# A Nystrom attention in front of a multiplicative FFN on one core: turnings from DMA and TensorE to VectorE, C v without zero blocks, other column blocks, another order

## The chip, the cores and the metric

The kernel runs on one core of a Trainium2 chip. The metric is device time in microseconds (us), from the first to the last instruction with what the runtime puts around them; lower is better. Engines are named as the profile names them: PE is TensorE (PEld its weight loads), DVE is VectorE, ACT is ScalarE, POOL is GpSimd, SP is SyncE, which here only issues transfers.

## The reference, cut to what matters

There are 8 batches of 8 heads, 576 tokens and 64 columns; 32 landmarks are means over 18 neighbouring tokens.

```python
q_lm = q.reshape(B, H, 32, 18, D).mean(axis=3)
k_lm = k.reshape(B, H, 32, 18, D).mean(axis=3)
A  = softmax(q    @ k_lm.T / 8)      # 576 x 32 for each head
Bm = softmax(q_lm @ k_lm.T / 8)      # 32 x 32
C  = softmax(q_lm @ k.T / 8)         # 32 x 576
Z = Bm.T / (norm_1(Bm) * norm_inf(Bm) + 1e-6)      # norms over rows and columns
for _ in range(6):
    Z = 2 * Z - Z @ Bm @ Z
x = (A @ Z @ C @ v)                  # heads side by side: 4608 x 512
out = ((x @ w1) * (x @ w2)) @ w3 @ w_out           # 512 -> 1024 -> 1024 -> 512, float32 out
```

## The kernel before, in words

**The dense half.** w3 and w_out are multiplied once, at the start, into one matrix w34 (1024 x 512). Both are split into a high and a low fp16 half (L303, L308, L324, L331) and three products are summed (`w34_mm`); w3 is turned beforehand by PE, four 128 x 128 blocks at a time (`w3_tr`, L317). x itself is never formed. For each batch the small matrix Z C v of each head is multiplied with w1 and w2 (`u_mm`, copied by `u_out`, L800), which gives u. Dense-1 (`d1_mm`) is then u times A, for 8 blocks j of 128 columns of the FFN and for 2 blocks of 288 tokens; ACT copies the first of the two products from PSUM (`d1_a`, L866) and DVE multiplies it with the second (`d1_b`, L872) into the tile ab. Dense-2 (`d2_mm`) multiplies ab with w34 for 128 tokens at a time, ACT copies the result out (L885) and SP stores it in four transfers (L895).

**The attention half.** It goes by quads, four heads of one batch, 16 in all. POOL's queue loads k and q as fp16 (`load_qk`, L391); SP turns the whole of it by a transposing DMA into the tile T (`trans`, L419). POOL sums the 18 tokens of each landmark in five steps (L427, L434) and scales the sum into a small tile with zero blocks (`mean_c`, L441, L445), which another transposing DMA turns (`lm_trans`, L452). PE then makes C's and Bm's scores in a bank of their own, psS (`s_mm`), and A's scores (`a_mm`: 40 matmuls of 128 rows, the landmarks standing in a matrix of which half is zero). C's maximum is shared between two halves of the partitions by a small matmul (`s_swap`), ACT makes its exponentials (L513), DVE turns them in blocks of 32 (L529), and POOL spreads the sums (L521). A goes through maximum, difference, exponential, sum and reciprocal (L555, L561, L570, L576, L577), POOL multiplies (L582), DVE turns it (L589) into the tile aT. Bm's scores are copied out (L489) and get a softmax of their own for each batch (L672 to L689). `cv_mm` multiplies C with v; v lies in a tile in which every second block of 64 columns is zero (`const_e` writes the zeros, L280, and `load_v` fills the others, L404). Five double steps of the iteration (`it_mm`, `it_out` L739) and three small products follow for each batch.

**The order of the work.** All instructions are tasks of a planner, the class `Plan`. It holds for each task an engine, an estimated duration, what it depends on, which slots of which rings of buffers it takes and frees, and a priority from a due time: `dense(b)` is 66 + 25.5 b, `att(n)` and `lane(b)` are derived from it. `run` makes a list schedule from these, and the kernel is written out in this order; each engine runs its own list strictly in order. The ring "P" has 6 of the 8 PSUM banks, psS has two. Nearly all matmuls are issued by the helper `mm` (L228), so they are told apart by their tiles. The tiles ab take the memory of the tiles of the w34 stage, so they begin when that is done.

Of the kernel before, what the change touches and what calls it, by code (L numbers as in the profile page):

```python
# [20 lines left out]
NC9 = 9  # L21
DM = 512
DF = 1024
HALF = 288
# [3 lines left out]
LOW = -1e30  # L28


class Task:
    def __init__(self, name, eng, dur, fn, deps, acq, rel, prio, mode, lat, move, after):
        self.name, self.eng, self.dur, self.fn = name, eng, dur, fn
        self.deps, self.acq, self.rel = deps, acq, rel
        self.prio, self.mode, self.lat, self.move, self.after = prio, mode, lat, move, after
        self.start = self.ready = None


class Plan:
# [3 lines left out]
    LAT = {"PE": 0.25, "ACT": 0.08, "DVE": 0.08, "POOL": 0.1, "SP": 0.0}  # L43
    SWITCH = 0.1
# [8 lines left out]
    def add(self, name, eng, dur, fn, deps=(), acq=(), rel=(), prio=0.0, mode=None, lat=None,  # L53
            move=0.0, after=0.0):
        t = Task(name, eng, dur, fn, list(deps), list(acq), list(rel), prio, mode,
                 self.LAT[eng] if lat is None else lat, move, after)
        self.by[name] = t
        self.tasks.append(t)
        return t

    def _slots(self, acq):

        got, when, taken = [], 0.0, {}
        for ring, key, n, uses in acq:
            free = self.rings[ring]
            used = taken.setdefault(ring, set())
            if n == 1:
# [3 lines left out]
                best = min(some, key=lambda i: (free[i], -(free[i ^ 1] is None) if ring == "P" else 0, i))  # L71
                pick = [best]
            else:
# [5 lines left out]
                best = min(some, key=lambda i: max(free[i], free[i + 1]))  # L79
# [5 lines left out]

    def run(self):
        free = {e: 0.0 for e in self.LAT}
        mode, moved = None, 0.0
        todo = list(self.tasks)
        waiting = {t.name: sum(1 for d in t.deps) for t in todo}  # L90
        after = {}
        for t in todo:
# [3 lines left out]
        for t in todo:  # L96
            if not waiting[t.name]:
                t.ready = 0.0
                avail[t.eng].append(t)
        order = []  # L100
        n = len(todo)
        while len(order) < n:
            best = None
            for e, cand in avail.items():
                opts = []
                for t in cand:
                    found = self._slots(t.acq)
                    if found is None:
                        continue
                    at = max(free[e], t.ready, found[0], t.after)  # L110
                    opts.append((at, t, found[1]))
                if not opts:
                    continue
                first = min(o[0] for o in opts)
                near = [o for o in opts if o[0] <= first + (0.05 if e == "PE" else 0.0)]
                at, t, got = min(near, key=lambda o: (
                    o[1].prio - (0.6 if e == "PE" and o[1].mode == mode else 0.0)))
                if best is None or at < best[0]:
                    best = (at, t, got)
            if best is None:  # L120
                left = [t.name for t in todo if t.start is None]
                raise RuntimeError(f"stuck with {len(left)}: {left[:12]} {self.rings}")
# [4 lines left out]
            dur = t.dur  # L127
            if e == "PE":
                if t.mode != mode:
                    dur += self.SWITCH  # L130
                mode = t.mode
            free[e] = at + dur
            end = at + dur + t.lat
            if t.move:
                moved = max(moved, at + dur) + t.move
                end = moved + t.lat
            t.end = end
# [5 lines left out]
            for key in t.rel:  # L143
                rec = self.left[key]
                rec[0] -= 1
                rec[1] = max(rec[1], end)
# [3 lines left out]
            for u in after.get(t.name, ()):  # L150
                waiting[u.name] -= 1
                if not waiting[u.name]:
                    u.ready = max(self.by[d].end for d in u.deps)
                    avail[u.eng].append(u)
            order.append(t)
        return order


@with_exitstack
def kernel(  # L160
# [18 lines left out]
    psS = banks[3]  # L179
# [8 lines left out]
    P.ring("P", 6)  # L188
    P.ring("S", 1)
    nats = slots(fixed, 4, [128, 2, GRP, D], FP16, "nat")  # L190
    Ts = slots(fixed, 3, [128, 2 * NC9, 128], FP16, "T")
    lsum = slots(fixed, 1, [128, 2, NC9, D], FP32, "ls")
    lm16 = slots(fixed, 2, [128, 3, 2, D], FP16, "lm")
    lmTs = slots(fixed, 3, [128, 3, 128], FP16, "lmT")
    vbs = slots(fixed, 4, [128, 2, 2, NC9, D], FP32, "vb")
    ecs = slots(fixed, 2, [128, 2, 2, 160], FP32, "ec")
    ecTs = slots(fixed, 4, [128, 2, 10, M], FP32, "ecT")
    eas = slots(fixed, 2, [128, GRP, M], FP32, "ea")
    ahs = slots(fixed, 2, [128, GRP, M], FP16, "ah")
    aTs = slots(fixed, 6, [128, S], FP16, "aT")  # L200
    uu = slots(fixed, 4, [128, 2, DF], FP16, "u")
    asb = slots(fixed, 4, [128, HALF], FP16, "asb")
    osb = slots(fixed, 4, [128, DM], FP32, "osb")
    bscs = slots(fixed, 2, [128, 2, 32], FP32, "bsc")
    wTs = slots(fixed, 2, [128, 2, 128], FP16, "wT")
    cvs = slots(fixed, 2, [128, 2, D], FP32, "cv")
    bms = slots(fixed, 2, [128, 2, 2, 32], FP32, "bm")
    xzs = slots(fixed, 4, [128, 2, 2, 32], FP32, "xz")
    zbs = slots(fixed, 2, [128, 2, 4, 32], FP32, "zb")
    tinies = slots(fixed, 8, [128, 48], FP32, "tiny")  # L210
# [6 lines left out]
    swapneg = fixed.tile([128, 2, 32], FP32, name="swapneg")  # L217
    blockones = fixed.tile([128, 128], FP32, name="blockones")
    ones = fixed.tile([128, 32], FP32, name="ones")
    maskS = fixed.tile([128, 2], FP32, name="maskS")  # L220
# [9 lines left out]


    T0 = 66.0
    PER = 25.5

    def dense(b):
        return T0 + PER * b

    def att(n):
        b, qd = divmod(n, 2)
        return max(2.0 + 6.0 * n, dense(b) - 46.0 + 13.0 * qd)  # L240

    def lane(b):
        return dense(b) - 19.0
# [9 lines left out]
    def const_c():  # L253
        nc.vector.memset(blockones, 0.0)
        nc.vector.memset(ones, 1.0)
        nc.vector.memset(swapneg, 0.0)
        nc.vector.memset(maskS, 0.0)
        for j in range(4):
# [6 lines left out]
            nc.vector.tensor_scalar(out=swapneg[r, 1 - j % 2, :], in0=ident[r, r], scalar1=-SCALE,  # L265
                                    scalar2=None, op0=ALU.mult)
        for s in range(2):
            nc.vector.memset(maskS[64 * s:64 * s + 64, s:s + 1], 1.0)
        for hp in range(2):
            nc.vector.memset(psS[:, 1, 160 * hp + 128:160 * hp + 160], LOW)  # L270

    def const_d():
        for t in lm16:
            nc.vector.memset(t, 0.0)

    def const_e(i):
        def fn():
            for t in vbs[2 * i:2 * i + 2]:
                for s in range(2):
                    nc.gpsimd.memset(t[64 * s:64 * s + 64, :, 1 - s, :, :], 0.0)  # L280
        return fn

    add("ca", "DVE", 0.3, const_a, prio=-10)
    add("cb", "POOL", 0.4, const_b, deps=["ca"], prio=-9)
    add("cc", "DVE", 3.0, const_c, deps=["cb"], prio=-8)
    add("cd", "DVE", 0.5, const_d, prio=-8.5)
    add("ce0", "POOL", 2.5, const_e(0), prio=14.0, after=6.0)
    add("ce1", "POOL", 2.5, const_e(1), deps=[f"wol{c}" for c in range(8)], prio=24.0)


    def load_wout(c):
        def fn():
            nc.sync.dma_start(out=wof[at(f"wf{c}")], in_=moe_w_out[128 * c:128 * c + 128, :])  # L293
        return fn

    def load_w3(j):
        def fn():
            nc.sync.dma_start(out=w3n[at(f"w3n{j}")], in_=moe_w3[128 * j:128 * j + 128, :])
# [13 lines left out]
    def w3_tr(j, h):  # L312
        def fn():
            ps = bank(at(f"ptr{j}{h}"))
            for i in range(4):
                c = 4 * h + i
                nc.tensor.transpose(out=ps[:, 128 * i:128 * i + 128],  # L317
                                    in_=w3n[at(f"w3n{j}")][:, 128 * c:128 * c + 128],
# [676 lines left out]
```

## Time and profile before

| what | value |
|---|---|
| median of three runs | 351.21 us (348.2 to 351.9) |
| span of the profiled execution | 343.6 us; the page gives no other time for it, so what lies around the span is taken from the median, 7.6 us |
| instructions in the profile | 10423, of them 4288 matmuls and as many weight loads |
| busy: PE, DVE, POOL, ACT | 277.7, 201.0, 154.2, 148.4 us |
| bytes moved | 48.39 MB, mean 141 GB/s |

A group of the profile reads: line, engine, operation, tile written <- tiles read, shape out <- shape in, count | busy us, mean ns of one | idle time of the engine just before, and what ended it. In the table by stage each line is a stretch (from:to in us), its length, and for each engine the busy us with the number of instructions, then the granted clock of PE, the share of the DMA engines and GB/s. Matmuls overlap in the records, so their pace is read from the starts in the timeline. A wait reads: who waited <- for whom: us in total, times, longest.

### The profile page before, as it was taken

Reading aid. Unit: us, or ns where it says so; the run is one execution under the profiler, and the core shown is the slowest. Engines: PE = TensorE matmul, PEld = TensorE weight load, DVE = VectorE, ACT = ScalarE, POOL = GpSimd, SP = SyncE. Lnnn points to the kernel's source line nnn. Section 1 sums busy time; section 2 is a strip of 40 time slices with the busy share of each in tenths; the row PEclk is TensorE's granted clock in tenths of the full one; section 3 lists DMA queues with packets and bytes.
Section 4 is the critical chain, followed back from the end, with each engine's and each line's share of the span. In section 5 each row is a group of like instructions: output and inputs, shape, how many; then the busy total and the mean of one; then the engine's idle time right before and its main releaser. Section 6 shows DMA issues by size and latency. Waiting matters only on the chain.

```text
span 343.6 us, 10423 instructions
## 1 busy us (share of the span) xinstructions
PE 277.7 (81%) x4288; PEld 152.7 (44%) x4288; DVE 201.0 (58%) x499; ACT 148.4 (43%) x349; POOL 154.2 (45%) x197
## 2 busy tenths in 40 slices
PE   3689888987738878897978899889898887997972
PEld 2244444633523534454535554544455444544531
DVE  7623546461987855684887487755867773432420
ACT  3522332405432344364526555653655255436432
POOL 6498594399783662655485583637011010000000
PEclk9999999999978969999999999999999999999998
DMA  8987989998897886369887997776541210221223
GB/s 214 358 184 152 220 223 207 178 195 177 133 220 82 144 187 129 73 128 192 180 161 169 188 190 144 173 156 138 126 108 32 56 39 3 60 65 32 60 62 93
DMA packets 64175, 48.39 MB, mean 141 GB/s; under 512 B 48256, under 2 KB 48256, under 8 KB 64128
## 3 DMA queue, kind: packets, MB, share of 16 engines
q1 hardware_dynamic: 58368, 36.19, 47.1%
q0 software_dynamic: 5760, 11.54, 20.8%
q8 instruction: 33, 0.54, 0.7%
q14 instruction: 14, 0.11, 0.1%
HBM read 38.80 MB, written 9.44 MB: 140 GB/s over the span
## 4 chain that ended last, share of the span: by engine, by line
PE 44%; DVE 19%; ACT 13%; DMA 11%; issue 5%; SPq 3%; POOL 3%; ACTq 0%; DVEq 0%; POOLq 0%
PE bank L228 44%; DVE ab L872 5%; ACT asb L866 4%; DMA nat<-in_q_dram 4%; ACT u L800 4%; DMA lmT<-lm 3%; DMA vb<-in_moe_w_out_dram 3%; ACT osb L885 2%; DMA vb<-in_v_dram 2%; POOL ls L427 1%; DVE xz L739 1%; DVE xz L722 1%; DVE bm L673 1%; ACT ec L513 1%; SPq L293 1%
## 5 line engine op out<-in xcount | busy, mean ns | idle before, releaser
L228 PE MATMUL bank<-aT,u 128*128 128x288 f16 x512 | 84.0, 291 | 17.2 <-DVE ab L872 8.0
L872 DVE TENSOR_TENSOR ab<-asb,bank 128x288 f16<-128x288 f16 x128 | 55.9, 447 | 56.5 <-ACT asb L866 31.9
L866 ACT CAST asb<-bank 128x288 f16<-128x288 f32 x128 | 49.9, 404 | 72.6 <-PE bank L228 59.9
L228 PE MATMUL bank<-w,ab 128*128 128x512 f16 x288 | 73.7, 382 | 3.5 <-ACT osb L885 1.2
L228 PEld LDWEIGHTS <-u 128*128 128x128 f16 x512 | 47.1, 98 | 48.4 <-issue 28.4
L228 PE MATMUL bank<-wo,w3t 128*128 128x512 f16 x192 | 48.9, 387 | 6.5 <-DVE w3t L331 3.8
L434 POOL TENSOR_TENSOR ls<-ls 128x512 f32<-128x512 f32 (+1 forms) x64 | 46.6, 728 | 4.5
L427 POOL TENSOR_TENSOR ls<-nat 128x1152 f32<-128x1152 f16 x16 | 37.8, 2366 | 20.6 <-DMA nat<-in_q_dram 20.0
L800 ACT CAST u<-bank 128x512 f16<-128x512 f32 x64 | 35.2, 598 | 19.1 <-PE bank L228 12.2
L228 PEld LDWEIGHTS <-ab 128*128 128x128 f16 x288 | 26.9, 98 | 29.0 <-issue 7.0
L885 ACT ACTIVATE osb<-bank 128x512 f32<-128x512 f32 x36 | 21.5, 598 | 30.3 <-PE bank L228 17.1
L582 POOL TENSOR_TENSOR ah<-ea,tiny 128x576 f16<-128x576 f32 x16 | 18.5, 1158 | 29.0 <-DVE tiny L577 21.2
L521 POOL TENSOR_TENSOR tiny<-tiny,maskS 128x4 f32<-128x4 f32 x16 | 3.2, 201 | 61.3 <-ACT ec L513 61.3
L228 PEld LDWEIGHTS <-w3t 128*128 128x128 f16 x192 | 17.8, 98 | 26.9 <-issue 9.7
L228 PE MATMUL bank<-xz 32*32 32x64 f32 (+1 forms) x768 | 20.5, 223 | 11.3 <-DVE xz L722 4.6
L228 PE MATMUL bank<-w,wT 64*32 64x512 f16 x512 | 22.8, 388 | 7.8 <-ACT u L800 2.2
L331 DVE SCALAR_TENSOR_TENSOR w3t<-bank,w3t 128x512 f16<-128x512 f32 x16 | 10.9, 685 | 27.1 <-ACT w3t L324 19.4
L228 PEld LDWEIGHTS bank<-xz 32*32 32x32 f32 x768 | 13.0, 108 | 28.2 <-issue 12.3
L739 DVE SCALAR_TENSOR_TENSOR xz<-xz,bank 128x128 f32<-128x128 f32 x40 | 11.4, 284 | 16.8 <-PE bank L228 16.0
L513 ACT ACTIVATE ec<-bank,tiny 128x320 f32<-128x320 f32 x32 | 16.8, 529 | 9.2 <-DVE tiny L506 8.9
L348 ACT ACTIVATE w<-bank 128x512 f16<-128x512 f32 x8 | 4.8, 596 | 35.0 <-PE bank L228 35.0
L228 PE MATMUL bank<-vb,ecT 128*32 128x128 f32 x576 | 18.0, 273 | 0.1
(75 smaller groups left out, 320.0 us busy)
## 6 DMA issues: line engine op xcount, KB each, us to landing
vb<-in_v_dram SPq DMA_DIRECT2D x64, 144.0 KB, 4.1
out_dram<-osb SPq DMA_DIRECT2D x144, 64.0 KB, 1.7
nat<-in_k_dram POOLq DMA_DIRECT2D x16, 288.0 KB, 5.3
nat<-in_q_dram POOLq DMA_DIRECT2D x16, 288.0 KB, 7.0
w3n<-in_moe_w_dram SPq DMA_DIRECT2D x8, 512.0 KB, 6.9
vb<-in_moe_w_out_dram SPq DMA_DIRECT2D x8, 256.0 KB, 8.6
w<-in_moe_w_dram POOLq DMA_DIRECT2D x8, 256.0 KB, 8.7
T<-nat SPq DMA_TRANSPOSE x16, 5.9
```

Source lines behind the costliest of these rows:

```text
L228: nc.tensor.matmul(out_, lhsT, rhs, start=start, stop=stop, **({} if pos is None else {"tile_position": pos}))
L331: nc.vector.scalar_tensor_tensor(out=t[:, 1, 512 * h:512 * h + 512], in0=bank(at(f"ptr{j}{h}")), scalar=WSC, in1=t[:, 0, 512 * h:512 * h + ...
L348: nc.scalar.activation(out=w34[:, j, :], in_=bank(at(f"pw{j}")), func=AXF.Copy, scale=1.0 / (WSC * WSC))
L427: nc.gpsimd.tensor_tensor(out=l, in0=nat[:, :, 0:9, :], in1=nat[:, :, 9:18, :], op=ALU.add)
L434: nc.gpsimd.tensor_tensor(out=l[:, :, x:x + m, :], in0=l[:, :, x:x + m, :], in1=l[:, :, y:y + m, :], op=ALU.add)
L513: nc.scalar.activation(out=ecs[at(f"ec{n}")][:, hp, :, :], in_=psS[:, :, 160 * hp:160 * hp + 160], func=AXF.Exp, scale=SCALE, bias=t[:, 2 ...
L582: nc.gpsimd.tensor_tensor(out=ahs[at(f"ah{n}")], in0=eas[at(f"ea{n}")], in1=tinies[at(f"ta{n}")][:, 0:18].unsqueeze(2).to_broadcast([128, ...
L739: nc.vector.scalar_tensor_tensor(out=new.rearrange("p s t x -> p (s t x)"), in0=xz.rearrange("p s t x -> p (s t x)"), scalar=2.0, in1=bank ...
L800: nc.scalar.copy(out=uu[at(f"u{b}{qd}")][:, wi, 512 * half:512 * half + 512], in_=bank(at(f"pU{b}{wi}{half}{qd}")))
L866: nc.scalar.copy(out=asb[at(f"as{b}{j}{ch}")], in_=bank(at(f"pD{b}{j}{ch}0"))[:, 0:HALF])
L872: nc.vector.tensor_mul(abs_[at(f"ab{b // 2}")][:, j, c0:c0 + HALF], asb[at(f"as{b}{j}{ch}")], bank(at(f"pD{b}{j}{ch}1"))[:, 0:HALF])
L885: nc.scalar.activation(out=osb[at(f"os{g}{t}")], in_=bank(at(f"pE{g}{t}")), func=AXF.Copy, scale=2.0 ** -12)
```

## The change

- **Turnings by VectorE.** q, k, the landmarks and A are turned by DVE in blocks of 32 x 32, and as pairs: two neighbouring fp16 values are taken as one 32-bit value. The two members of a pair (index e) lie side by side afterwards, so S and A are made by two matmuls each, one for each e, of 32 rows, with operands of step 2. No transposing DMA is left. w3 is turned by DVE too, before it is split, from SBUF; its loads become four transfers a block.
- **Scores.** Bm's scores are made as a 19th group of A's, and take A's softmax; the copy and the softmax for each batch go. A is 152 matmuls of 32 rows and columns. The tile psS goes, and the ring "P" has all 8 banks.
- **C v.** v has no zero blocks; the 72 matmuls of a batch have 64 rows and 64 columns. The zeroing and POOL's spreading of sums go.
- **Landmark scaling** moves from POOL to ACT.
- **Dense-1** takes 192 tokens (three blocks a batch), both products in one bank; ab is four tiles of 384 tokens; a store is two transfers.
- **Order.** The planner has other durations, a model of transfers, and due times from two tables of numbers.

The diff, cut to its core:

```diff
-    P.ring("P", 6)
-    P.ring("S", 1)
+    P.ring("P", 8)
...
-    vbs = slots(fixed, 4, [128, 2, 2, NC9, D], FP32, "vb")
+    vbs = slots(fixed, 4, [128, 2, NC9, D], FP32, "vb")
...
     def w3_tr(j, h):
         def fn():
-            ps = bank(at(f"ptr{j}{h}"))
-            for i in range(4):
-                c = 4 * h + i
-                nc.tensor.transpose(out=ps[:, 128 * i:128 * i + 128],
-                                    in_=w3n[at(f"w3n{j}")][:, 128 * c:128 * c + 128],
-                                    identity=ident[:, :])
+            nc.vector.transpose(
+                out=w3f[at(f"w3f{j}")][:, 4 * h:4 * h + 4].rearrange("p e g i -> p (e g i)"),
+                in_=w3n[at(f"w3n{j}")][:, :, 128 * h:128 * h + 128]
+                .rearrange("p g (e x) -> p e g x", x=32))
...
-    def trans(n):
-        def fn():
-            nc.sync.dma_start_transpose(
-                out=Ts[at(f"T{n}")][:, :, :],
-                in_=nats[at(f"nat{n}")].rearrange("p t r d -> p (t r d)"))
+    def trans(n, t):
+        def fn():
+            nc.vector.transpose(
+                out=Ts[at(f"T{n}")][:, t].rearrange("p r l e -> p (r l e)").bitcast(FP32),
+                in_=nats[at(f"nat{n}")][:, t].rearrange("p r d -> p (r d)").bitcast(FP32))
...
     def mean_c(n):
         def fn():
...
+            nc.scalar.activation(out=lm16[at(f"lm{n}")], in_=lsum[at(f"ls{n}")][:, :, 0, :],
+                                 func=AXF.Copy, scale=1.0 / GRP)
...
     def lm_trans(n):
         def fn():
-            nc.sync.dma_start_transpose(
-                out=lmTs[at(f"lmT{n}")][:, :, :],
-                in_=lm16[at(f"lm{n}")].rearrange("p a e d -> p (a e d)"))
+            nc.vector.transpose(
+                out=lmTs[at(f"lmT{n}")].rearrange("p t l e -> p (t l e)").bitcast(FP32),
+                in_=lm16[at(f"lm{n}")].rearrange("p t d -> p (t d)").bitcast(FP32))
...
     def s_mm(n):
...
+            for e in range(2):
+                for hh in range(4):
+                    hp, h2 = divmod(hh, 2)
+                    r = slice(32 * hh, 32 * hh + 32)
+                    for t in range(2):
+                        o = 64 * (h2 ^ qd) + 32 * t
+                        mm(ps[o:o + 32, hp, 0:288], lm[r, 1, :, e],
+                           T[r, 0, 9 * t:9 * t + 9, :, e].rearrange("p r l -> p (r l)"),
+                           start=(e == 0), stop=(e == 1), pos=(32 * hh, o))
...
     def a_mm(n):
...
+            for g in range(GRP + 1):
+                for e in range(2):
+                    for hh in range(4):
+                        r = slice(32 * hh, 32 * hh + 32)
+                        w = lm[r, 1, :, e] if g == GRP else T[r, 1, g, :, e]
+                        mm(ps[r, g, :], w, lm[r, 0, :, e], start=(e == 0), stop=(e == 1),
+                           pos=(32 * hh, 32 * hh))
...
+    def b_norm(n):
+        def fn():
+            b, qd = divmod(n, 2)
+            nc.vector.tensor_tensor(
+                out=bms[at(f"bm{b}")][:, 0, qd, :], in0=eas[at(f"ea{n}")][:, GRP, :],
+                in1=tinies[at(f"ta{n}")][:, GRP:GRP + 1].to_broadcast([128, M]), op=ALU.mult)
...
     def cv_mm(b):
...
             for c in range(NC9):
...
+                for qd in range(2):
+                    n = 2 * b + qd
+                    for hh in range(4):
+                        hp, h2 = divmod(hh, 2)
+                        r, o = slice(64 * (h2 ^ qd), 64 * (h2 ^ qd) + 64), 32 * hh
+                        mm(ps[o:o + 32, qd, 0:D], ecTs[at(f"ecT{n}")][r, hp, c, :],
+                           vbs[at(f"vb{n}")][r, hp, c, :], start=(c == 0), stop=(c == 8),
+                           pos=(r.start, o))
...
     def d1_mm(b, j, ch):
         def fn():
...
+            ps = d1_ps(b, j, ch)
             for wi in range(2):
-                ps = bank(at(f"pD{b}{j}{ch}{wi}"))
                 for qd in range(2):
-                    mm(ps[:, 0:HALF], uu[at(f"u{b}{qd}")][:, wi, 128 * j:128 * j + 128],
-                       aTs[at(f"aT{2 * b + qd}")][:, cols], start=(qd == 0), stop=(qd == 1))
+                    mm(ps[:, wi, :], uu[at(f"u{b}{qd}")][:, wi, 128 * j:128 * j + 128],
+                       aTs[at(f"aT{2 * b + qd}")][:, CH * ch:CH * ch + CH],
+                       start=(qd == 0), stop=(qd == 1))
...
+        self.prio = ANCHOR[anchor] + off + OFF.get(kind, 0.0)
```

More of the change, by code (lines that the diff above doesn't have):

```diff
@@ L21 @@
 NC9 = 9
+RP = GRP // 2
 DM = 512
 DF = 1024
-HALF = 288
+CH = 192
 X64 = 64.0
@@ L84, in _slots, with _move @@
         return when, got
+    def _move(self, at, queue, size):
+        load, (a, b) = self.load, ("SP", "POOL")
+        gone = max(0.0, at - self.moved)
+        self.moved = max(self.moved, at)
+        both = min(load[a], load[b], gone / 2.0)
+        load[a] -= both
+        load[b] -= both
+        rest = gone - 2.0 * both
+        for x in (a, b):
+            less = min(load[x], rest)
+            load[x] -= less
+            rest -= less
+        load[queue] += size
+        other = b if queue == a else a
+        return load[queue] + min(load[queue], load[other])
     def run(self):
         free = {e: 0.0 for e in self.LAT}
-        mode, moved = None, 0.0
-        todo = list(self.tasks)
-        waiting = {t.name: sum(1 for d in t.deps) for t in todo}
+        self.load, self.moved = {"SP": 0.0, "POOL": 0.0}, 0.0
+        mode = None
+        waiting = {t.name: len(t.deps) for t in self.tasks}
         after = {}
-        for t in todo:
+        for t in self.tasks:
             for d in t.deps:
@@ L151, in run @@
                 waiting[u.name] -= 1
+                same = t.eng == u.eng and not t.dma
+                u.ready = max(u.ready, t.free + self.SELF[e] if same else t.end)
                 if not waiting[u.name]:
-                    u.ready = max(self.by[d].end for d in u.deps)
                     avail[u.eng].append(u)
@@ L865, in fn @@
         def fn():
-            nc.scalar.copy(out=asb[at(f"as{b}{j}{ch}")], in_=bank(at(f"pD{b}{j}{ch}0"))[:, 0:HALF])
+            nc.scalar.copy(out=asb[at(f"as{b}{j}{ch}")], in_=d1_ps(b, j, ch)[:, 0, :])
         return fn
```

680 lines of the change are left out of this document (298 added, 382 removed), and 14 rows, old and new, of tables (ANCHOR, OFF).

## The prediction

> **What bounds the kernel now.** I read the page's head first, then a table by stage, then the costliest groups, the waits, and the timeline for the pace of TensorE (PE). All times come from one profiled execution: 343.6 us of span. The three runs have a median of 351.21 (348.2 to 351.9), so 7.6 us lie around the span; I add the same 7.6 to the new sum.
>
> ```profile
> span 343.6 us, 10423 instructions
> PE 277.7 (81%) x4288; PEld 152.7 (44%) x4288; DVE 201.0 (58%) x499; ACT 148.4 (43%) x349; POOL 154.2 (45%) x197
> ...
> q1 hardware_dynamic: 58368, 36.19, 47.1%
> q0 software_dynamic: 5760, 11.54, 20.8%
> ```
>
> No engine is full. PE's 277.7 us count overlapping ends, so I cut the run into stages: up to the first product on VectorE (DVE), up to the last turning of A, and the rest; and two short pieces.
>
> ```profile
> core 0: us, PE busy (x) PEld busy (x) DVE busy (x) ACT busy (x) POOL busy (x), PEclk, DMA share, GB/s
> 0.00:87.00 87.00, 67.57 (x796) 34.28 (x796) 42.89 (x102) 29.92 (x59) 61.04 (x79) 1.00 0.98 211
> 87.00:282.60 195.60, 162.34 (x3034) 93.10 (x3038) 140.02 (x352) 92.68 (x231) 93.13 (x119) 0.97 0.71 137
> 282.60:343.60 61.00, 47.84 (x468) 25.36 (x458) 18.05 (x46) 25.86 (x59) 0.00 (x0) 0.99 0.21 53
> 98.00:106.00 8.00, 4.04 (x64) 2.07 (x64) 6.67 (x18) 0.40 (x1) 3.93 (x7) 0.60 1.17 186
> 123.00:131.00 8.00, 6.54 (x76) 2.88 (x64) 3.73 (x9) 4.50 (x11) 4.15 (x5) 0.57 1.00 217
> ```
>
> Stage 1 is bound by DMA (share 0.98, DVE half idle) and passes only three quads (a quad is four heads of a batch). Stage 2 has no bound: DVE 72% busy, and twice PE starves and its granted clock falls to about 0.6. Stage 3 is PE work. The true pace of PE is start to start:
>
> ```profile
> 31.93 0.49 PE L228 MATMUL bank<-lmT,T 128*32 128x64 f16 x40
> 188.12 2.24 PE L228 MATMUL bank<-vb,ecT 128*32 128x128 f32 x72
> 288.44 1.63 PE L228 MATMUL bank<-aT,u 128*128 128x288 f16 x12 [0.47 <-DVE xz L739]
> 332.22 5.34 PE L228 MATMUL bank<-w,ab 128*128 128x512 f16 x24 [0.69 <-ACT osb L885]
> ```
>
> Taking off the length of the last one (0.193, 0.273, 0.286, 0.379 us), a start comes every 7.6, 27.7, 122 and 216 ns. By these, stage 2 holds 372 x 0.122 + 192 x 0.216 = 87 us of dense work and about 58 of attention and changes of tile mode (some 110 of 0.12, below): 145 in 195.6, 74%.
>
> ```profile
> L872 DVE TENSOR_TENSOR ab<-asb,bank 128x288 f16<-128x288 f16 x128 | 55.9, 447 | 56.5 <-ACT asb L866 31.9 <-PE bank L228 20.6 <-ACT osb L885 1.4
> L529 DVE STREAM_TRANSPOSE ecT<-ec 128x640 f32<-128x640 f32 x16 | 13.4, 835 | 1.6 <-ACT ec L513 1.4
> L331 DVE SCALAR_TENSOR_TENSOR w3t<-bank,w3t 128x512 f16<-128x512 f32 x16 | 10.9, 685 | 27.1 <-ACT w3t L324 19.4 <-PE bank L317 4.1 <-PE bank L228 3.2
> L673 DVE TENSOR_TENSOR bm<-bsc,tiny 128x64 f32<-128x64 f32 x8 | 4.9, 618 | 0.3
> L780 DVE TENSOR_TENSOR wT<-bank,wT 128x128 f16<-128x128 f32 x8 | 2.3, 291 | 0.3
> L691 DVE STREAM_TRANSPOSE bm<-bm 128x64 f32<-128x64 f32 x8 | 2.0, 245 | 0.3
> ```
>
> These rows price DVE: 245 ns for a turning of 64 columns, 835 for 640, so 1.02 ns a column: 768 for 576, 475 for 288. A product takes 291 ns at 128 columns and 447 at 288: 355 at 192.
>
> ```profile
> POOL tiny L521 <- ACT ec L513: 61.3, 14, 10.4
> POOL ls L427 <- DMA nat<-in_q_dram: 20.0, 7, 6.1
> ```
>
> GpSimd (POOL) stood 61.3 us in its queue before a 0.2 us step, and 20.0 for q.
>
> **The change, part by part.**
>
> DMA. 16 large and 16 small turnings go: 128 x (2304 + 384) x 2 bytes x 16 = 11.0 of q1's 36.2 MB, in most of its 58368 packets. The time is unknown from 11.0/36.2 of q1 (47.1% of 343.6 = 162 us: 49) to 92 (if the other 25 MB went at 358 GB/s, the best of the page's 40 slices). I take 70 us of DMA time. It stops being the bound of stage 1; it earns nothing elsewhere.
>
> DVE, over the run. Added: 32 turnings of q and k (24.6), 16 of landmarks (3.9), 16 of w3 (0.70 each, 11.2), 16 small products for B (0.19, 3.0). Changed: products 192 x 0.355 = 68.2 against 57.2; A by pairs 7.6 against 12.3; C's softmax 576 for 640 columns (-2.0); 19 for 18 groups (+1.6). Gone: B's copy and softmax (16.4). That is 201 + 32 = 233 us busy; all 581 instructions of the new list, each by its row and without regard to overlap, make 242. An instruction that waits for nothing starts some 0.08 before its forerunner's end (at 184.50 the 0.29 of L780, at 184.71 the next), so 242 can pass in 195.
>
> DVE against POOL. L673 reads two SBUF tensors; its fastest is 224 ns, its mean 618: 0.39 lost at POOL's work. The low halves of w3 (L331) read PSUM now and SBUF afterwards, 16 more such steps; with B's products and two of the iteration there are 48: 48 x 0.39 = 19 us, 0 if POOL idles, 48 x 2.37 (one L427) = 114 at worst. I take 19, 9 of them in stage 1 and 8 in stage 2. The Trainium skill, "GPSIMD Engine Reference" (its table of specifications), says that GpSimd shares SBUF interfaces with VectorE and contends with instructions of two SBUF inputs; this trace agrees (224 against 618 ns), and the rule speaks against this edit.
>
> PE. Zero blocks: 72 records of 27.7 ns a batch become 144 of half the columns on twice the array tiles. Bounds 6.9 and 27.7 ns; I take 7.6, the pace of A, 1.1 for 2.0 us: -7. w3's transposes leave: 64 x 0.14 = -9. A: 152 matmuls of 32 columns a quad for 40 of 64; between 3.8 ns (half the columns) and 7.6; I take 6: 0.9 us for 0.3, +10. Dense-1: 768 x 0.0815 = 512 x 0.122, nothing; if a weight load (98 ns each) no longer hides, +12. Changes between full and small array tiles fall from 178 to 44 in the instruction order, 0.12 each (176.64 after 176.28 where 16 starts need 0.23): -16. Net -22.
>
> ACT gets 192 casts at 0.32 for 128 at 0.404 (+10) and 16 landmark scalings (0.27, +4): about 160 of 305 us, hidden beside DVE. The scaling waits for POOL, and behind it in ACT's queue stand the casts for which DVE's products wait; the nearest price is L521, 61.3/16 = 3.8 us each. I take nothing, since POOL would run ahead; 61 us is the other end, which is the third rival's case. POOL loses 16.8 (L441, L445), 8.5 of zeroing, and the wait of 61.3. The waits for q and k move to DVE's queue: whatever is behind, the products and so PE's banks, waits too.
>
> **The sum by stages**, with the instructions of the new order.
> - Stage 1 (to the first product): 175 DVE instructions, 82.7 us by rows, 69 nose to tail, now for seven quads and not three; PE needs 59. Start 4.7, POOL 9: 83 to 96, 73 without POOL. I take 85.
> - Stage 2 (to the last turning of A): 314 DVE instructions, 128 by rows, 103 nose to tail, and 8 for POOL; PE 480 x 0.0815 + 160 x 0.216 + 29 = 103. Bounds: 111, and 164 if DVE and PE together pack as loosely as now, (136 + 103) x 195.6/(140 + 145). I take the middle, 138: PE used at 75%, as now (74%), and DVE's 111 nose to tail at 80%.
> - Stage 3: 288 x 0.0815 + 128 x 0.216 + 12 = 63 of PE, and 6 after the last matmul as now: 69; with the slack of now's stage (43 in 55), 87. I take 74.
> 85 + 138 + 74 + 7.6 = 304.6, **305 us**.
>
> **Rivals.**
> - *It packs tightly*: 78 + 118 + 70 + 7.6 = 274. For: in 290 to 312 PE already runs almost without gaps. Against: DVE's 111 nose to tail would fill 94% of stage 2.
> - *Loads late*: DVE now stands for q and k as POOL did (20.0): stage 1 is 105, 325 us. For: 23 MB must come first. Against: the turnings freed the queues.
> - *DVE's queue is the new bound* (the other side): its in-order waits stay, 72% busy in stage 2: 136/0.72 = 189, so 356, slower. It decides from there: above 72% it is faster. For: the 56.5 us before L872. Against: eight banks for six, one a product.
> - *Small matmuls start no faster than C's records*, every 27.7 ns: A costs 4.2 us a quad, +53, of which stages 1 and 2 (59 and 103 of PE, +23 and +26) hide two thirds beside DVE: 305 + 18 = 323. Against: the row of 7.6.
> The Trainium skill, "TensorE: Matmul & The Clock Gate" ("Wait — 56ns, not 53.3ns?"), states that starts never come closer than about 25 ns; by that (an estimate) A would cost 3.8 us a quad. This trace disagrees: 7.6 ns on four array tiles.
>
> **How the numbers follow.** Forecast 0.58, tight 0.17, late loads 0.13, DVE's queue 0.08, small matmuls 0.04. About 1% (3.5 us) can be told from no change: faster 0.90, same 0.03, slower 0.07. Range 274 to 338: left out are the lower half of the tight case, DVE's queue and the forecast's own upper tail, together less than 0.2.
>
> **What would show it.** First product near 85 us after seven quads; DVE near 235 us and over 80% busy in the middle; q1 near 25 MB; A's 152 starts within 1.2 us; no piece with the clock at 0.6. A first product after 105, or DVE at 72% in the middle with waits before the products, would make me wrong.

## The result: 438.1 us, a quarter slower

The changed kernel takes 438.13 us (median of four runs, 433.41 to 441.58), the kernel before, measured beside it, 351.55: a ratio of 1.239 (95% interval 1.227 to 1.252). 304.6 was forecast. The ratios here and below are of the means of the faster executions alone; two of these four, the profiled one among them (span 438.9, time 440.6), were over 1.5% longer than the fastest and are left out of it.

From the page's head of the changed kernel:

```profile
span 438.9 us, 15303 instructions
PE 302.1 (69%) x6752; PEld 190.6 (43%) x6752; DVE 222.5 (51%) x579; ACT 155.3 (35%) x421; POOL 124.1 (28%) x137
...
PEclk9999979969565699999596877997779679999999
...
q1 hardware_dynamic: 16544, 25.18, 22.4%
q0 software_dynamic: 5696, 11.54, 15.7%
q8 instruction: 53, 0.87, 0.8%
```

q1 moves 25.18 MB, as forecast, and DVE is busy for 222.5 us, for 233. No engine is fuller than before, and all of them stand longer. Two rows are new: PE's clock is below full in 16 of 40 slices (before in four), and q8, which the prediction never looked at, has 53 packets of 16 KiB for 33.

The same three stages as before (to the first product, to the last turning of A, the rest), then two stretches of the start:

```profile
core 0: us, PE busy (x) PEld busy (x) DVE busy (x) ACT busy (x) POOL busy (x), PEclk, DMA share, GB/s
0.00:154.80 154.80, 86.14 (x2190) 48.66 (x2191) 79.58 (x175) 36.88 (x80) 63.22 (x73) 0.84 0.55 121
154.80:358.00 203.20, 152.00 (x3780) 100.98 (x3777) 115.24 (x314) 78.96 (x231) 60.91 (x64) 0.85 0.34 74
358.00:438.90 80.90, 64.01 (x803) 40.98 (x787) 27.66 (x93) 39.49 (x110) 0.00 (x0) 0.96 0.20 47
10.00:18.00 8.00, 0.00 (x0) 0.00 (x0) 1.53 (x3) 1.26 (x2) 6.45 (x7) 1.00 0.26 90
28.00:38.00 10.00, 0.00 (x0) 0.00 (x0) 1.39 (x2) 1.89 (x3) 0.00 (x0) 1.00 0.49 138
```

154.8, 203.2 and 80.9 us stand against 85, 138 and 74: 70, 65 and 7 too long. The last two rows lie before PE's first matmul: the DMA engines, freed of the turnings, run at a quarter and at a half (at 0.83 between the two).

What PE waited for, in the changed kernel (us in total, times, longest):

```profile
PE bank L275 <- issue: 49.6, 22, 5.0
PE bank L275 <- ACT w3t L347: 40.3, 1, 40.3
PE bank L275 <- DVE ab L848: 13.3, 20, 2.0
```

The kernel before has 0.3 us in the first of these rows. "Issue" means that PE stood, and nothing in the profile held it: no semaphore, no buffer. PE's timeline shows one such place, in a quad's A:

```profile
126.08 2.23 PE L275 MATMUL bank<-vb,ecT 64*32 64x64 f32 x141
...
129.56 0.25 PE L275 MATMUL bank<-tiny,unit 64*32 64x1 f32 x11 [1.20 <-issue]
129.75 1.10 PE L275 MATMUL bank<-lmT,T 32*32 32x32 f16 x117
133.84 0.37 PE L275 MATMUL bank<-lmT,T 32*32 32x32 f16 x27 [3.00 <-issue]
```

117 matmuls start within 0.9 us (every 7.9 ns, near the row of 7.6 that the forecast used), then PE stands for 3.0 us in the middle of a run with all operands there. Beside it I put the trace's records of q8. A packet holds 16 KiB, and 53 packets for PE's 13504 matmuls and weight loads are one for 256 of them, 64 bytes each. The number follows PE's instructions from run to run: 33 for 8576 in the kernel before, 43 for 11072 in e3 below, 35 for 8896 in e5. So these are pages of PE's own program. Counting 256 started matmuls and weight loads to a page, the first page 56 short, with which the boundaries fall on the waits (the first and the last column are good to a few tenths of a us):

```
kernel, fetch     last page entered   next asked for   landed    its first instruction
after, 12th           129.62              131.22        132.44        133.90
after, 16th           148.81              149.79        150.78        152.26
after, 36th           293.67              294.85        295.77        297.29
before, 12th          135.32              136.96        137.86        146.90
```

Over the 21 pages of the changed kernel whose first instruction came within 3.1 us of the request, the medians are: asked for 1.0 us after PE entered the page before, first instruction 2.5 us after that (it lands 0.9 to 1.5 us after the request), in all 3.6 us from page to page. A page that lasts 10 us, the mean of the kernel before, does not show it: 0.3 us of such waits there. A's 304 instructions use up a page in 1 us. Of the 49.6 us, 26.7 stand before A's matmuls:

```profile
L275 PE MATMUL bank<-lmT,T 32*32 32x32 f16 x2304 | 24.3, 180 | 26.9 <-issue 26.7
```

The Trainium skill, "Runtime: NRT & Kernel Launch" ("Instruction fetch mechanics"), has the pages of 256 instructions and says that crossing into one is mostly hidden; the trace agrees on the size, and not on the hiding, here.

The start has another cause. Before, PE begins on w3 at 4.76 us and on the products with W_out at 7.39; now at 40.28, when ScalarE has split the block of w3 that PE waits for:

```profile
40.28 10.05 PE L275 MATMUL bank<-wo,w3t 128*128 128x512 f16 x31 [40.28 <-ACT w3t L347]
```

### The profile page after: what moved, and what is told of

The parts are those of the page before. It is cut to its first block, busy times and chain, and to the rows that moved or that the text cites. A ratio compares the mean times of both kernels' runs of the same rounds, so it can differ in the third digit from the quotient of the medians.

```text
span 438.9 us, 15303 instructions
## 1 busy us (share of the span) xinstructions
PE 302.1 (69%) x6752; PEld 190.6 (43%) x6752; DVE 222.5 (51%) x579; ACT 155.3 (35%) x421; POOL 124.1 (28%) x137
## 3 DMA queue, kind: packets, MB, share of 16 engines
q1 hardware_dynamic: 16544, 25.18, 22.4%
## 5 line engine op out<-in xcount | busy, mean ns | idle before, releaser
L848 DVE TENSOR_TENSOR ab<-asb,bank 128x192 f16<-128x192 f16 x192 | 59.5, 348 | 61.8 <-ACT asb L842 44.8
L275 PE MATMUL bank<-aT,u 128*128 128x192 f16 x768 | 79.0, 255 | 16.4 <-ACT asb L842 7.2
L275 PE MATMUL bank<-w,ab 128*128 128x512 f16 x288 | 76.8, 413 | 7.3 <-DVE ab L848 3.1
L275 PEld LDWEIGHTS <-u 128*128 128x128 f16 x768 | 67.5, 101 | 29.3 <-issue 18.4
L842 ACT CAST asb<-bank 128x192 f16<-128x192 f32 x192 | 53.5, 325 | 52.6 <-PE bank L275 33.3
L447 POOL TENSOR_TENSOR ls<-nat 128x1152 f32<-128x1152 f16 x16 | 38.3, 2397 | 60.2 <-ACT lm L460 37.3
L275 PE MATMUL bank<-lmT,T 32*32 32x32 f16 x2304 | 24.3, 180 | 26.9 <-issue 26.7
L509 ACT ACTIVATE ec<-bank,tiny 128x288 f32<-128x288 f32 x32 | 15.8, 499 | 53.3 <-DVE tiny L501 47.4
L275 PEld LDWEIGHTS <-T 32*32 32x32 f16 x2304 | 21.9, 90 | 29.3 <-issue 28.7
L439 DVE STREAM_TRANSPOSE T<-nat 128x576 f32<-128x576 f32 x32 | 24.0, 754 | 0.0
L275 PE MATMUL bank<-vb,ecT 64*32 64x64 f32 x1152 | 17.1, 262 | 5.7 <-issue 5.0
```

Source lines behind the costliest of these rows:

```text
L275: nc.tensor.matmul(out_, lhsT, rhs, start=start, stop=stop, **({} if pos is None else {"tile_position": pos}))
L439: nc.vector.transpose(out=Ts[at(f"T{n}")][:, t].rearrange("p r l e -> p (r l e)").bitcast(FP32), in_=nats[at(f"nat{n}")][:, t].rearrange(" ...
L447: nc.gpsimd.tensor_tensor(out=l, in0=nat[:, :, 0:9, :], in1=nat[:, :, 9:18, :], op=ALU.add)
L509: nc.scalar.activation(out=ecs[at(f"ec{n}")][:, hp, :], in_=banks[at(f"pS{n}") // 2][:, hp, 0:288], func=AXF.Exp, scale=SCALE, bias=t[:, 2 ...
L842: nc.scalar.copy(out=asb[at(f"as{b}{j}{ch}")], in_=d1_ps(b, j, ch)[:, 0, :])
L848: nc.vector.tensor_mul(abts[at(f"ab{i // 2}")][:, j, CH * (i % 2):CH * (i % 2) + CH], asb[at(f"as{b}{j}{ch}")], d1_ps(b, j, ch)[:, 1, :])
```

## The experiments

Times are medians of four runs or more; the ratio is to the kernel before, measured beside each, with its interval; the last column is PE's "issue" row. The edits are given in short, words standing for code in some lines.

| run | us | ratio | PE waits for issue |
|---|---|---|---|
| changed kernel | 438.1 | 1.239 (1.227-1.252) | 49.6, 22 times |
| e1 W_out by rows | 428.2 | 1.219 (1.210-1.228) | 53.9, 22 |
| e2 before, W_out's new pattern | 365.5 | 1.043 (1.037-1.049) | |
| e3 half of A | 403.8 | 1.148 (1.140-1.156) | 27.6, 15 |
| e4 hand order | 436.9 | 1.245 (1.239-1.251) | 48.6, 25 |
| e5 A wide | 382.2 | 1.090 (1.081-1.098) | 15.4, 9 |
| e6 A wide, W_out by rows | 375.2 | 1.074 (1.066-1.082) | 14.7, 9 |
| e7 A in two bursts (and e1) | 431.3 | 1.230 (1.220-1.239) | 53.4, 27 |
| e8 dense filling in A | 444.3 | 1.270 (1.263-1.277) | 30.8, 19 |
| e9 w3 first (and e1) | 426.4 | 1.202 (1.189-1.215) | |
| e10 measured costs (and e1) | 424.0 | 1.198 (1.189-1.207) | |
| e11 e6 and dense filling | 387.0 | 1.095 (1.086-1.104) | 12.6, 9 |
| e12 e6, normalising on DVE | 386.1 | 1.088 (1.077-1.099) | |
| e13 e6 in the hand order | 378.1 | 1.071 (1.060-1.083) | |
| e14 e6 without q's turnings | 373.0 | 1.057 (1.047-1.067) | |
| e15 e6 with half of dense-2 | 355.4 | 0.998, without interval (1.007 by the medians) | |
| e16 e6 with short means | 372.3 | 1.056 (1.046-1.066) | |
| e17 before, sums on DVE | 351.5 | 1.008 (1.003-1.012) | |
| e18 e17, scaling on ACT | 363.1 | 1.044 (1.037-1.050) | |

**The load of W_out (e1, e2, e9).** The change loads W_out so that a chunk holds four groups of 32 rows that lie 256 rows apart.

```
e1, in the changed kernel               e2, in the kernel before
-in_=moe_w_out.rearrange(               -in_=moe_w_out[128*c:128*c+128, :]
-  "(a e c) f -> e a c f", ...)[c]      +in_=moe_w_out.rearrange(
+four loads of 32 rows, [256*a+32*c:     +  "(a e c) f -> e a c f", a=4, e=8)[c]
+  256*a+32*c+32, :]
```

> The changed kernel; only the load of W_out is undone in its pattern: 32 transfers of 32 neighbouring rows (64 KB) for 8 of four groups of 32 rows (256 KB). Theory L (the four-group pattern moves at a quarter of the DMA: 102 GB/s and a share of 0.26 from 10 to 18 us, against 344 GB/s and 1.08 in the kernel before): the transfers land in about 10 us for 36, the first product of W_out and w3 starts near 20 us for 40.3, the first product of dense-1 near 133 for 154.8, and the time falls by about 20 us to 410-422. Rival O (the late start is hidden, since the order waits elsewhere): within 5 us of 438. Rival S (it is SyncE's issuing, not the pattern): 32 issues of 0.43-0.7 us make it no faster, 430-445.

> The kernel before; only its 8 loads of W_out take the changed kernel's pattern (four groups of 32 rows each, so that the rows of W_out meet the wrong rows of w3: the output differs). Theory L: the DMA share falls from 1.0 to some 0.3-0.6 in the first 18 us, W_out lands 10 us or more later, and 10 to 20 us are added: 361-372. Rival (pattern does not matter, or the start is hidden): 348-355.

The stretch from 10 to 18 us, in e1 and then in e2 (the kernel before has a DMA share of 1.08 and 344 GB/s there):

```profile
10.00:18.00 8.00, 0.00 (x0) 0.00 (x0) 7.77 (x25) 3.15 (x5) 6.41 (x9) 1.00 0.65 139
```

```profile
10.00:18.00 8.00, 3.42 (x7) 0.74 (x8) 2.37 (x4) 2.37 (x4) 0.00 (x0) 1.00 0.26 100
```

The same pattern gives the same share, 0.26, at 90 and 100 GB/s, in both kernels: four engines' worth of sixteen, the number of groups. In the kernel before it costs 14 us (15 by the ratios); in the changed one, undoing it brings 10 (7 by the ratios), half of what theory L had or less, and PE then starts at 28.4 and not at 20: w3 comes behind W_out in SyncE's queue, from 18.3 us on. The Trainium skill, "DMA: Bandwidth & Descriptors" ("Why a DMA increments its semaphore by 16 and not by 1"), has this rule: a transfer is spread over the largest number of engines, up to 16, that divides its outermost dimension on both sides. The trace agrees, for four.

e9 also puts two loads of w3 ahead of W_out's in that queue (due times of those two set to the lowest).

> The whole computation; W_out by blocks of 32 rows, and the first two loads of w3 ahead of W_out's in SyncE's queue (in the run with the load alone TensorE still starts at 28.4 us, against 7.4 in the kernel before). Theory L2 (the rest of the late start costs as it did there): TensorE starts at 13-18 and the time falls from 428 to 415-422. Rival (from here on something else sets the pace): 424-432.

PE starts at 16.4, but the first product comes at 140.3 for 141.4, and the time falls by 2 us (by the ratios by 6). The rival holds, by the time as by the first product: from there on something else sets the pace.

**The pages of A (e3, e5, e6, e7, e8).**

```
e3:  -for e in range(2):                     # of a_mm: one of two halves of the feature pairs
     +for e in range(1):
e5:  -152 matmuls of 32 columns              # a_mm: other numbers, all that follows is done on them
     +for x, m in ((0, 512), (512, 96)):
     +    for hh in range(4): mm(pf[r, x:x+m], lm[r, 1, :, 0], tf[r, x:x+m], ...)
e7:  -A{n}: groups 0 to 18
     +A{n}_0: groups 0 to 9;  A{n}: groups 10 to 18, 2.5 us later in the planner's timetable
e8:  +if g == 9: ten mm(pf[:, 608:1024], tf[:, 0:128], tf[:, 128:544])
```

> The changed kernel with the second half of the pairs left out of A's and B's scores: 76 matmuls a quad for 152 (the scores are of half the features). Theory F (TensorE runs its instructions off 16 KiB pages of 256, whose fetch ends 2 to 3 us after the burst has used up the page before): 1216 matmuls and as many weight loads, 9.5 of 53 pages, are gone, and a burst of 152 instructions no longer uses up a page, so most of the 22 waits of 2.25 us in A go: 25 to 45 us less, 393-413. Theory P (the matmuls' own pace): 1216 x 7.9 ns = 9.6 us at most, 428-438.

> The changed kernel, but the 152 matmuls of a quad's A and B scores are replaced by 8 wide ones (512 and 96 columns a head; the scores are other numbers, everything behind them is done on them). 4608 of 13504 instructions of TensorE go, 18 of 53 pages, and no burst uses up a page. Theory F (fetch waits, 53 us of them in 22 places): nearly all waits go, the clock falls to half for far less than the 118 us of now, and the time falls by 55 to 85 us, to 353-383. Theory P (the matmuls' own pace, 1.2 us a quad): 16 us, 420.

> The same, and W_out loaded by blocks of 32 neighbouring rows as well. If fetch and load are all that is wrong, this ends near the forecast: 305 to 330. If the order or a further cost is at work too, 340-375.

> The whole computation: W_out by blocks of 32 rows, and A's 152 matmuls in two bursts of 80 and 72, with 2.5 us between them in the planner's timetable for other work of TensorE (its timetable ends at 283 for 263). Theory F: a burst of 160 instructions seldom crosses a second page before the fetch has come, the waits of 56 us in the run with the load alone fall to some 25, and the time to 395-412 from 428. Theory P: 10 to 20 us longer than 428, by the timetable.

> The changed kernel with extra work: ten dense matmuls of 416 columns, whose results nobody reads, in the middle of each quad's A (some 1.8 us, 28 us of TensorE in all). Theory F: they run while the next page comes, the clock stays up longer, and the time stays within 10 of 438 or falls. Rival (A costs its pace, and TensorE is short of time): 20 to 30 us longer, 458-468.

e3 and e5 tell the theories apart: half of A's matmuls bring 34 us where their pace has 10, and wide ones bring 56 (53 by the ratios) where it has 16. The 8 wide matmuls and e3's 76 stream the same 2432 columns a quad, for 4864 before, and yet e5 is 22 us faster than e3: so it is the number of instructions that costs, and the "issue" row falls with them (49.6, 27.6, 15.4). Two other things change with the instructions. The mean granted clock rises (0.87, 0.90, 0.93), and no run parts what that is worth from the waits. And e5's A no longer reads the turned q; but among PE's waits in the changed kernel, down to 0.4 us, is none for that tile.

e8 adds about 28 us of dense work to PE and takes 6 us longer (11 by the ratios), while the "issue" row falls by 19 (49.6 to 30.8): about two thirds of the added work runs in the time that PE stood for its pages. Here too the clock rises, from 0.87 to 0.93.

The pages are not gone in e6: PE still stands 14.7 us in 9 places, most of it before C v's matmuls.

```profile
L275 PE MATMUL bank<-vb,ecT 64*32 64x64 f32 x1152 | 17.6, 257 | 10.0 <-issue 9.2 <-DVE ecT L518 0.7
```

A batch of C v is now 144 matmuls, 288 instructions, more than a page; the kernel before has half as many and no such wait.

e7 failed as I had laid it out. Its PE timeline shows why:

```profile
165.99 0.84 PE L275 MATMUL bank<-lmT,T 32*32 32x32 f16 x80
167.21 0.42 PE L275 MATMUL bank<-xz 32*32 32x64 f32 x16 [0.37 <-DVE xz L721]
167.45 0.24 PE L275 MATMUL bank<-lmT,T 32*32 32x32 f16 x12
170.16 0.58 PE L275 MATMUL bank<-lmT,T 32*32 32x32 f16 x52 [2.46 <-issue]
```

The 2.5 us were a gap in the planner's timetable alone. On the chip the second burst follows the first after 16 other matmuls; I take it that PE is late there and what was to fill the gap is done or not ready. The waits are 53.4 us, as without the split (53.9 in e1), and the theory that they follow the pages is neither helped nor hurt by it.

**The order (e4, e10, e13).** e4 and e13 replace the searched tables by the due times of the kernel before; e10 corrects the planner's costs.

```
e4, e13:  -ANCHOR = {...searched...}; OFF = {...}
          +a{n}: max(2 + 6 n, 20 + 25.5 (n // 2) + 13 (n % 2)); l{b}: 47 + 25.5 b
          +d{i}: 66 + 8.5 i; w{j}: 4 + 6.6 j; OFF = {}
e10:      -A 0.6, C v 1.02, issuing W_out 0.5
          +A 2.4, C v 2.2, issuing W_out 1.9
```

> The changed kernel, all of its operations, with the due times of the kernel before (six quads at 6 us, then 25.5 us a batch; all offsets zero) for the searched tables. By the planner's own timetable this order ends at 290 and the searched one at 263. Theory O (the searched order fits its own timetable so closely that late loads and waiting TensorE spoil it: GpSimd stands 112.5 us before A's normalising): 395-425, faster than 438. Theory C (operations cost what they cost, the order is no worse than another): 27 us slower, as the timetable has it, 450-470.

> The whole computation, W_out by blocks of 32 rows; the planner is told what the traces show: 2.4 us for a quad's A (0.6 in the code), 2.2 for a batch's C v (1.02) and 1.9 for SyncE's issuing of a block of W_out (0.5). Its timetable then ends at 303 for 263, in another order. Theory O (engines stand in their queues because the order counts on bursts that TensorE cannot keep): 400-415 for 428. Theory F alone (the waits come wherever the bursts stand): 422-435.

> The run with A by 8 wide matmuls and W_out by rows (375 us), in the order of the kernel before's due times. Theory O (without the fetch waits it is the searched order that spoils the rest): 345-362. Rival (the order does not matter, as it did not with the fetch waits: 437 against 438): 368-382, or longer by the 27 us of the timetables, 400.

Two quite different orders give the same time, with all of the pages' waits (437 and 438) and with fewer of them (378 and 375), though one is 27 us shorter by the planner's own timetable. Better costs bring 4 to 7 us. None of the three orders gets back what the change lost; the searched gain is not to be seen on the chip either.

**What is left (e11, e12, e14, e15, e16).** Each changes one thing in e6. e14 leaves out the turnings of q, e15 every second product of dense-2, e16 three of the means' four adding steps; in these three all else keeps its order.

```
e11: +ten mm(pf[:, 608:1024], tf[:, 0:128], tf[:, 128:544]) behind each quad's A
e12: -nc.gpsimd.tensor_tensor(out=ahs..., op=mult)     +nc.vector.tensor_tensor(...)
e14: -trans(n, 1)                                      # DVE, 16 x 0.75 us
e15: -for c in range(4*h, 4*h+4):                      +for c in range(4*h, 4*h+4, 2):
e16: -for x, y, m in ((0,4,4), (0,2,2), (0,1,1), (0,8,1)):   +((0,8,1),)
```

> The run with A by 8 wide matmuls and W_out by rows (375 us, clock at half for 69 us of its span) and ten dense matmuls of 416 columns behind each quad's A, whose results nobody reads: 28 us of added work, 20 instructions a quad. Theory G (the low clock between dense stretches costs as much as the work missing there): half clock falls below 40 us and the time stays within 8 of 375 or falls. Rival (TensorE's own work counts): 390-403.

> The same run (375 us), with A's normalising on VectorE for GpSimd, which stood 77 us in its queue ahead of it, with the means of later quads behind. Theory Q (GpSimd's queue order delays the quads): the means come early, 355-368. Rival (VectorE's work counts more: 16 x 0.7 us added): 378-390.

> The run of 375 us without the 16 turnings of q (0.75 us each, 12 us of VectorE; the wide matmuls do not read them), all else in the same order. If VectorE's queue bounds (68% busy in the middle, and in-order): 10 to 18 us less, 357-365. If not: 370-376.

> The run of 375 us with half of dense-2's products left out: 144 matmuls of 0.216 us, 31 us of TensorE, all else in the same order. If TensorE's dense work bounds the middle and the end (133 of 168 us busy, 65 of 81): 22 to 31 us less, 344-353. If the waits of the other engines do: 362-372.

> The run of 375 us with three of the four adding steps left out of the means (some 2.5 us a quad, 40 us of GpSimd; the landmarks are other numbers), all else in the same order. If GpSimd's chain bounds the first part: 8 to 20 us less, 355-367. If not: 370-376.

By the medians (by the ratios in brackets): 12 us of turnings less on DVE bring 2 (6), though its busy time falls by 5.4 only; 40 us less of POOL's bring 3 (6), and normalising on DVE, 22 us more of its busy time, costs 11 (5). The ratios are good to about 1%, 3.5 us. 31 us less of PE's bring 20 (26), 28 us more cost 12 (8). So two thirds or more of the dense work that e15 takes out lay on the path, but less than half of what e11 adds, some of which falls into PE's waits; of DVE's work a part lies there, of POOL's little. Against the forecast e6 is late in every stage:

```profile
0.00:124.30 124.30, 75.98 (x1181) 39.27 (x1182) 80.81 (x174) 36.64 (x80) 64.58 (x73) 0.85 0.70 150
124.30:291.80 167.50, 132.66 (x2453) 85.83 (x2455) 113.47 (x314) 78.86 (x231) 60.93 (x64) 0.94 0.41 89
291.80:373.20 81.40, 65.08 (x838) 41.83 (x823) 27.62 (x93) 39.49 (x110) 0.00 (x0) 0.94 0.20 47
```

39, 29 and 7 us over. No single run owns them. That PE and DVE wait for each other in a looser pack than I took is my reading, and no run shows it alone.

**Two parts in the kernel before (e17, e18).** The 61.3 us that GpSimd stood for ScalarE, and the scaling of the landmarks.

```
e17: -nc.gpsimd.tensor_tensor(out=t[:, 8:12]...)       +nc.vector.tensor_tensor(...)
e18: -nc.gpsimd.tensor_scalar(out=lm..., 1/18) x2      +nc.scalar.activation(out=lm..., scale=1/18) x2
```

> The kernel before; the 0.2 us step that GpSimd waited 61.3 us for (L521) is done by VectorE. Theory R (the wait was worth something, as the sum has it): GpSimd's means come earlier, 338-346. Rival (the first part is bound by the transfers, the middle by TensorE; a wait of an idle engine): 349-354.

> The same, and the scaling of the landmarks (16.8 us of GpSimd) by ScalarE, as in the changed kernel. Theory R: 333-343. Rival: 348-355, or longer where ScalarE now stands for GpSimd with casts behind it.

What GpSimd waited for, longest first, in e17:

```profile
POOL ah L582 <- DVE tiny L577: 64.2, 11, 16.5
POOL ls L427 <- DMA nat<-in_q_dram: 32.1, 7, 7.2
```

and two rows from e18, and two from the changed kernel:

```profile
POOL ls L427 <- DMA nat<-in_q_dram: 35.4, 5, 7.7
...
POOL ls L427 <- ACT lm L444: 18.0, 4, 6.5
```

```profile
POOL ah L564 <- DVE tiny L559: 112.5, 11, 23.8
POOL ls L447 <- ACT lm L460: 37.3, 5, 23.2
```

In e17 the wait is gone and stands at the next step of the queue instead (21.2 us before, now 64.2): GpSimd had time, and nothing was gained. e18 costs 12 us beyond e17. The sums of the means have one buffer; GpSimd may not begin the next quad's until the scaling has read it, and the scaling now stands in ScalarE's queue behind casts that wait for PE. e17 has no such wait, e18 has 18.0 us of it, and the changed kernel 37.3. ScalarE's own work, which grows by 6 us in e18, is the other thing that could cost time; the run does not part the two.

## Why the prediction was wrong, point by point

Two steps failed. The price of A is the one that the runs show; the packing, further down, is the larger one, and its cause stays open.

- **A, "152 matmuls of 32 columns a quad for 40 of 64 ... I take 6: 0.9 us for 0.3, +10".** This is the first step that failed. The pace came out near my upper bound (7.9 ns; 1.2 us a quad for the 0.9 I took). But a burst is priced by its instructions as well as its starts, and the sum had no term for that: 304 of them outrun the fetch, PE stands 2.3 us each time (49.6 in 22), and the program has 20 more pages. Taken out, A is worth 53 to 56 us (e5), of which its pace explains 16. My rival of 4.2 us a quad, 0.04, had nearly the right price with another cause; it let two thirds of it hide behind DVE, where little of it hid.
- **The 25 ns between starts,** from the Trainium skill, "TensorE: Matmul & The Clock Gate" ("Wait — 56ns, not 53.3ns?"), which I set aside for a row of 7.6: within a page the trace still disagrees, starts come every 7.9 ns. But a long stream of small matmuls did not keep that: where PE waited, a page of 128 pairs of weight load and matmul took 3.6 us, 28 ns a pair. A row of 40 matmuls could not show it.
- **"They stop bounding stage 1."** The transfers' volume did fall as said, and DMA's share in stage 1 from 0.98 to 0.55. It earned nothing: the new load of W_out uses a quarter of the engines, and PE starts 33 us later. I costed the bytes of the loads that stay and not their new pattern. Its price is 7 to 10 us here (e1; e5 against e6) and 14 in the kernel before (e2).
- **Late loads, as a rival,** I had put on q and k, at 105 us for the first product. It was right in kind and named the wrong transfer.
- **"The scaling waits for POOL ... I take nothing, since POOL would run ahead."** The wait that shows is the other way round: POOL waits for the scaling, through the one buffer of the sums (18.0 us in e18). Moving the scaling costs 12 us in the kernel before (e18 against e17), this wait and ScalarE's added work together.
- **"The wait of 61.3 gone."** True, and worth nothing (e17): a wait of an engine that has time moves on to its next step.
- **Clock.** "No piece with the clock at 0.6" was wrong: the mean granted clock is 0.87 (0.85 over the first two stages), and the busy share alone does not keep it up. In e6 PE is busy for two thirds of a stretch and has 0.57; in the kernel before, from 80 to 100 us, it is busy for as large a share (13.33 of 20) and has 0.99:

```profile
90.00:124.30 34.30, 23.04 (x704) 16.01 (x704) 21.20 (x59) 9.59 (x26) 17.41 (x21) 0.57 0.71 145
```

Of its 704 matmuls 13 are dense products, the rest small ones. The Trainium skill, "TensorE: Matmul & The Clock Gate" ("Part 1: The HAM clock gate"), has the clock follow how busy PE has been over windows of 3.4 us. Whether the small tiles or the gaps between them bring it down in this stretch, no run here shows. What the low clock costs was not separated: adding 28 us of dense work to e6 raised the clock from 0.91 to 0.95 and cost 12 (8 by the ratios).
- **C v, -7:** nothing by its pace. 141 starts take 2.23 us, every 14 ns, twice as many records at half the interval. And it was given no price for its 288 instructions a batch, before which PE stands 9.2 us in e6.
- **Dense-1 by 192 columns, nothing:** right. 16 matmuls in 1.48 us (less the last one's 0.255) are 82 ns each, the weight loads hidden:

```profile
400.02 1.48 PE L275 MATMUL bank<-aT,u 128*128 128x192 f16 x16 [0.35 <-ACT osb L862]
```

- **DVE** at 233 us was 222.5, but 57% in the middle and not over 80%. The rival that ends slower had DVE's queue as the bound at 72%; its sign came true and its mechanism did not (16 turnings fewer are worth 2 to 6 us). DVE against POOL, taken at 19 us over 48 steps, came out smaller: the 32 steps of L354 and L574 took 11 us over their fastest (928 ns for 649, 550 for 146).
- **The packing,** "PE used at 75%, as now": this is the second step that failed. In e6, with A's bursts and W_out's pattern gone, the 103 us of PE's work in stage 2 fill 61% of 167.5, stage 1 is 39 us over, and 70 us remain between 375 and 305. PE's waits for pages are 14.7 of them, most before C v, and PE starts at 28.6, though e9's earlier start brought only 2 to 6. The rest has no single owner. The runs show what it is not: neither of the other orders, and little of GpSimd's or VectorE's load by itself. That PE and DVE wait in turn for short serial steps, with fewer dense runs to fill the gaps, is my reading; no run shows it alone.
- **Around the span** lie 1.7 us and not 7.6 (440.6 and 438.9 of one execution); the rest was the difference between executions.

Of 133 us, then, A's matmuls explain 53 to 56 (against the 10 that the sum had for them), W_out's pattern 7 to 10, and some 70 remain, of which C v's pages and the scaling on ScalarE may have a part. The causes of more than half of the miss are open.

## What to carry to other kernels

Count instructions, not only columns: a matmul costs two with its weight load, and where 256 of them would pass in less than the 3.6 us that a page took here, expect PE to stand for its own program; give such work fewer, wider instructions. Before a load is rearranged, look at the outermost dimension of its pattern, and at what it does to the DMA share. A wait of an engine that has time was worth nothing here, and a step that is moved to another queue takes its buffers' next users along.

## What the hardware showed that I had not expected

- PE's program comes in pages of 16 KiB. Where PE waited (21 pages), the next was asked for 1.0 us after the last one was entered, and from page to page it took 3.6 us, by the medians; the waits are 49.6 us for 0.3 in the kernel before.
- A transfer of 256 KB whose outermost dimension is 4 ran at 90 to 100 GB/s with a DMA share of 0.26, in two kernels; in the changed one SyncE then stood 7.1 us at the fifth of them and 2.5 at each further one, with every load behind it.
- With PE two thirds busy, mostly on small array tiles, the granted clock was 0.57 (e6), for 0.99 at the same busy share in the kernel before.
